# A gated convolution on one core: rows of T nine partitions apart, z in two blocks, output columns 8 bytes apart, three gate buffers

## The chip, the cores and the metric

The kernel runs on one core of a Trainium2 chip. The metric is the device time of one execution in microseconds. Three runs of the kernel before took 737.18 to 741.06 us, the median is 739.61 us. The profile is of one execution that took 739.31 us.

## What is computed

A softmax over seven taps gives, for each batch, position and head, the weights of a short causal filter over x. The filtered x goes through a gated block: a five-tap filter per channel and a sigmoid make the gate, one matrix product makes the value, and a second matrix product follows their product. x is 8 x 4224 x 192, with 8 heads of 24 channels; everything is float32, the three weights of the block come as float64.

```python
w = np.exp(weight_gen - np.max(weight_gen, axis=-1, keepdims=True))   # [B, S, H, 7]
w = w / (np.sum(w, axis=-1, keepdims=True) + 1e-09)
x_unf = x_pad[:, np.arange(S)[:, None] + np.arange(7)[None, :], :].reshape(B, S, 7, H, 24)
a = np.einsum('bshk,bskhg->bshg', w, x_unf).reshape(B, S, D)
gate_pre = np.zeros((B, S, D))
for k in range(5):
    gate_pre += conv_w[k][None, None, :] * ap[:, k:k + S, :]           # ap: a, 4 zero rows ahead
gate = 1.0 / (1.0 + np.exp(-gate_pre))
return gate * (a @ w_val) @ w_out
```

## The kernel before

The first filter is done on TensorE. For a group of 120 positions and one head and batch, the output is x (126 rows by 24 channels, held in 32 columns) times a band matrix T (126 rows by 120 positions) whose diagonals are the softmax weights. The sequence of 4224 positions is cut into 36 groups (88, 34 times 120, 56); pair 0 is the first group, pairs 1 to 17 are two groups each, pair 18 is the last group.

T is built by DMA. A `Softmax` part handles some 500 positions of all batches: weights are loaded into `wt` (`load`, L200), then max (L209), sub (L213) on VectorE (DVE), exp (L217) on ScalarE (ACT), sum, reciprocal and norm (L221 to L244) on DVE. `halo` (L236) copies the next rows' weights beside each partition's own, `spread` (L255) writes the taps on ACT into `zt`, and `store` (L261) writes rows with zeros behind them into a DRAM block `z`, cleared earlier by `clear` (L180). `load_t` (L299) reads from z with a row step that is a little shorter than the row, so that the band comes out slanted, one window of 16 rows at a time, into `tb`. x goes into `xt` by `load_x` (L278).

Per pair q, TensorE does: `bank` (L324), 8 banks of products for the two groups, into PSUM buffers `ps0` and `ps1`; then, for the pair before, the value product with the gate's half in four lines (`wvm_` L393, `wva_` L398, `wvd_` L401, `wvb_` L406); and for the pair before that the output product (`omA` L423, `omB` L432) into `ps3`, `ps1` and `ps2`. ACT evicts the banks to `ringA`, `ringB` and `S` (`evac`, L339), makes the gate's first tap (`tap0`, L365), the sigmoid (`sigm`, L374) and the output copies (`oev`, L441). DVE does the other taps (L369) and the product of gate and value (`gv`, L413 and L416). GpSimd (POOL) issues the small copies from S into holes of the rings (`move`, L347 and L349) and, from the third pair on, the x loads. SyncE (SP) issues the T loads, weights, halo, z and output stores.

Each engine works in order. The order is a table: `at(t, fn, ...)` gives a call a nominal time, and the calls are emitted in the order of these times. `when(q)` is the nominal start of pair q. Two `tb` buffers (one for each group of a pair), three `xt` buffers, and two gate buffers `aA`, `aB` set how far ahead work may run.

Of the kernel before, what the change touches and what calls it, by code (L numbers as in the profile page):

```python
# [16 lines left out]
def tile_dynconv_gated_moe(  # L17
# [245 lines left out]
    class Group:  # L263
# [16 lines left out]
        def segments(self):  # L280
            f = self.s - PAD
            for j in range(-(-self.k // G)):
                for i, p in enumerate(parts):
                    lo = max(G * j, p.use - f)
                    hi = min(G * j + G, self.k, ([q.use for q in parts] + [S])[i + 1] - f)
# [412 lines left out]
```

## Time and profile before

| | us |
|---|---|
| median of three runs | 739.61 |
| profiled execution | 739.31 |
| its span, first to last instruction | 737.5 |
| TensorE (PE) busy with matmuls | 556.2 (75%) |
| VectorE (DVE) busy | 417.4 (57%) |
| ScalarE (ACT) busy | 355.3 (48%) |
| GpSimd (POOL) busy | 186.4 (25%) |
| mean busy share of the 16 DMA engines, pairs 4 to 17 | 0.73 |

PE's share is an average over a start with long idle stretches and a steady part. In the rows below a line `L324 PE` is a group of matmuls, `PEld` the loads of their weights. A bracket behind a row of the timeline is the idle time of that engine just before it and what ended it. [...]

### The profile page before, as it was taken

The numbers are of one execution on the slowest core, as the hardware profiler recorded it, in microseconds if no ns is written. First come the engines' busy times: TensorE is split into PE (matmuls) and PEld (weight loads), VectorE is DVE, ScalarE is ACT, GpSimd is POOL, SyncE is SP. The second block draws the span as 40 slices with busy tenths as digits, with TensorE's granted clock in tenths as the row PEclk, the third lists the DMA queues.
The fourth block names the chain that finished last, engine by engine and source line by source line (L and its number), as shares of the span: only waits on it lengthen the run. The fifth ranks groups of instructions, "written<-read, shape, count | busy, mean of one in ns | idle before, by whom it ended". The sixth has DMA issues, their size and how long they took to land.

```text
span 737.5 us, 15169 instructions
## 1 busy us (share of the span) xinstructions
PE 556.2 (75%) x6444; PEld 443.5 (60%) x6444; DVE 417.4 (57%) x309; ACT 355.3 (48%) x433; POOL 186.4 (25%) x297
## 2 busy tenths in 40 slices
PE   4023503659689968996899995998699779999986
PEld 2022403447569666875587784767587658687675
DVE  3341351767367837692777455874587457836650
ACT  2321613625474556546564726374645474582432
POOL 9335210224040404040404312230314030403300
PEclk8556656779989988998999997999799979999989
DMA  8699696996856876787779692969388948873223
GB/s 260 123 217 200 162 209 170 209 219 104 231 107 173 186 205 121 195 163 191 138 198 178 187 226 53 206 133 258 97 182 158 253 88 182 191 201 82 61 81 99
DMA packets 67021, 123.47 MB, mean 167 GB/s; under 512 B 15625, under 2 KB 41684, under 8 KB 66954
## 3 DMA queue, kind: packets, MB, share of 16 engines
q1 hardware_dynamic: 52282, 90.29, 50.6%
q0 software_dynamic: 13936, 31.91, 21.0%
q8 instruction: 51, 0.84, 0.5%
q10 hardware_dynamic: 736, 0.32, 0.2%
q14 instruction: 16, 0.13, 0.1%
HBM read 60.83 MB, written 48.29 MB: 148 GB/s over the span
## 4 chain that ended last, share of the span: by engine, by line
PE 38%; DMA 28%; ACT 10%; issue 9%; SPq 6%; DVE 6%; POOL 2%; ACTq 0%; DVEq 0%; POOLq 0%
PE ps L423 11%; DMA wt<-in_weight_gen_dram 11%; PE ps L324 10%; DMA tb<-z 9%; PE ps L432 6%; SPq L299 5%; PE ps L398 4%; DMA xt<-in_x_dram 3%; ACT ot L441 3%; ACT aA L365 3%; ACT S L339 2%; PE ps L393 2%; DVE mx L209 2%; PE ps L401 2%; PE ps L406 2%
## 5 line engine op out<-in xcount | busy, mean ns | idle before, releaser
L324 PE MATMUL ps<-tb,xt 126*32 126x120 f32 (+2 forms) x4608 | 201.0, 340 | 170.0 <-DMA tb<-z 76.3
L324 PEld LDWEIGHTS ps<-tb,xt 126*32 126x32 f32 (+2 forms) x4608 | 180.3, 131 | 188.8 <-issue 80.5
L369 DVE SCALAR_TENSOR_TENSOR aA<-ringA,wf,aA 128x1920 f32<-128x1920 f32 (+2 forms) x76 | 158.0, 2079 | 137.1 <-ACT aA L365 135.2
L349 POOL DMA_DIRECT2D ringB<-S x76 | 42.3, 561 | 442.9 <-ACT ringB L339 424.5
L441 ACT COPY ot<-ps 120x768 f32<-120x768 f32 (+2 forms) x72 | 83.2, 1164 | 145.1 <-PE ps L432 73.7
L423 PEld LDWEIGHTS ps<-wf,aA 128*120 128x120 f32 (+2 forms) x576 | 130.3, 309 | 10.3 <-issue 7.3
L423 PE MATMUL ps<-wf,aA 128*120 128x192 f32 (+2 forms) x576 | 135.2, 388 | 0.7 <-DVE aA L413 0.7
L347 POOL DMA_DIRECT2D ringA<-S x152 | 82.1, 546 | 24.7 <-DMA ringB<-S 21.3
L369 DVE SCALAR_TENSOR_TENSOR aB<-ringB,wf,aB 128x960 f32<-128x960 f32 (+2 forms) x76 | 86.9, 1144 | 2.0
L432 PE MATMUL ps<-wf,aB 64*120 64x192 f32 (+2 forms) x576 | 76.6, 394 | 3.1 <-ACT ot L441 3.1
L209 DVE TENSOR_REDUCE mx<-wt 128x256 f32<-128x1792 f32 (+3 forms) x11 | 20.1, 1828 | 101.1 <-DMA wt<-in_weight_gen_dram 101.1
L432 PEld LDWEIGHTS ps<-wf,aB 64*120 64x120 f32 (+2 forms) x576 | 67.6, 302 | 15.9 <-ACT ot L441 7.9
L398 PE MATMUL ps<-ringA,wva 128*128 128x480 f32 (+2 forms) x144 | 61.8, 571 | 0.0
L255 ACT COPY zt<-wt 128x384 f32<-128x384 f32 (+6 forms) x44 | 39.1, 968 | 41.2 <-DMA wt<-wt 41.2
L413 DVE TENSOR_TENSOR aA<-ps,aA 128x960 f32<-128x960 f32 (+2 forms) x36 | 39.3, 1130 | 30.7 <-ACT ot L441 30.7
L365 ACT ACTIVATE aA<-ringA,wf 128x960 f32<-128x960 f32 (+2 forms) x38 | 50.3, 1326 | 9.8 <-DMA ringA<-S 9.7
L339 ACT COPY ringA<-ps 128x480 f32<-128x480 f32 (+2 forms) x72 | 37.8, 576 | 33.9 <-PE ps L324 33.9
L374 ACT ACTIVATE aA<-aA 128x1920 f32<-128x1920 f32 (+2 forms) x19 | 32.0, 1686 | 37.3 <-DVE aA L369 37.2
L398 PEld LDWEIGHTS ps<-ringA,wva 128*128 128x128 f32 x144 | 25.8, 189 | 36.2 <-issue 22.5
L217 ACT ACTIVATE wt<-wt 128x1792 f32<-128x1792 f32 (+3 forms) x11 | 16.4, 1493 | 41.0 <-DVE wt L213 40.9
L393 PE MATMUL ps<-ringA,wvm 128*32 128x480 f32 (+2 forms) x288 | 32.5, 560 | 0.9 <-ACT ot L441 0.9
L406 PE MATMUL ps<-ringB,wvb 64*128 64x480 f32 (+2 forms) x144 | 31.6, 555 | 0.0
(60 smaller groups left out, 387.7 us busy)
## 6 DMA issues: line engine op xcount, KB each, us to landing
out_dram<-ot SPq DMA_DIRECT2D x68, 360.0 KB
xt<-in_x_dram POOLq DMA_DIRECT2D x30, 768.0 KB, 10.4
tb<-z SPq DMA_DIRECT2D x208, 88.0 KB
z<-zt SPq DMA_DIRECT2D x8, 1152.0 KB
wt<-in_weight_gen_dram SPq DMA_DIRECT2D x16, 448.0 KB
z<-tb SPq DMA_DIRECT2D x2, 2944.0 KB
wt<-wt SPq DMA_DIRECT2D x9, 588.0 KB
ringA<-S POOLq DMA_DIRECT2D x136, 30.0 KB, 5.2
```

The costliest lines, as they stand in the source:

```text
L324: nc.tensor.matmul(out=pa[Q * c:Q * c + Q, n * l:n * l + n], lhsT=g.xb[0:k, LH * u + l, C * h:C * h + Q], rhs=g.t[0:k, u, PAD // 2:(PAD + ...
L339: nc.scalar.copy(out=dst, in_=pa)
L347: nc.gpsimd.dma_start(out=ringA[q:q + h, LH * u:LH * u + LH, p0:p0 + n], in_=St[p:p + h, :, 0:n])
L349: nc.gpsimd.dma_start(out=ringB[HD * u + q:HD * u + q + h, :, p0:p0 + n], in_=St[p:p + h, :, 0:n])
L365: nc.scalar.activation(out=self.acc(g)[:, ls], in_=self.src(g, 0)[:, ls], func=AF.Copy, scale=cw[:, g, 0:1])
L369: nc.vector.scalar_tensor_tensor(out=a, in0=self.src(g, j), scalar=cw[:, g, j:j + 1], in1=a, op0=ALU.mult, op1=ALU.add)
L393: nc.tensor.matmul(out=self.v2(e)[c:c + Q], lhsT=wvm[:, Q * i:Q * i + Q], rhs=self.A(e, u), start=True, stop=False, tile_position=(0, c))
L398: nc.tensor.matmul(out=self.v01(e)[:, u], lhsT=wva, rhs=self.A(e, u), start=True, stop=False)
L406: nc.tensor.matmul(out=self.v01(e)[:, u], lhsT=wvb[hs], rhs=self.Bt(e)[hs], start=False, stop=True, tile_position=(HD * u, 0))
L423: nc.tensor.matmul(out=ps[b][0:n, u, D * t:D * t + D], lhsT=g[:, u, 2 * k + t], rhs=woa, start=first and t == 0, stop=not first, skip_grou ...
L432: nc.tensor.matmul(out=ps[b][0:n, u, D * t:D * t + D], lhsT=g[hs, 2 * k + t], rhs=wob[hs], start=first and t == 0, stop=not first, skip_gr ...
L441: nc.scalar.copy(out=self.ot(e)[0:n, :, 2 * D * k:2 * D * k + 2 * D], in_=ps[b][0:n, :, 0:2 * D])
```

## The change

T's window becomes 14 rows, nine windows a group, and row i of window w goes to partition 9 i + w; x goes to the same partitions, by one DMA for each of the 8 batches. A cell of T (the weights of two positions for 4 batches and 8 heads) has 272 bytes for 256. The blocks in DRAM are two, each for one part at a time, of 64 x 8 rows for each half of the batches, and are cleared from a tile of zeros. The two halves of the batches lie on odd and even partitions in the softmax. There are three gate buffers, and `tap0` and the ring's halo stand in the pair's own stage. The banks run group by group. The two positions of an output product are neighbours, so that its weights' columns are 8 bytes apart for 16; an output store moves 1536 bytes a row for 3072. The table of times is new.

```diff
-    CELL = 2 * W
+    CELL = 2 * W + 4
+    HC2 = CELL // 2
-    G = 16
+    G, NW = 14, 9
...
-    tb = [const.tile([P, 2, CELLS, LH, H, 2], FP32, name=f"tb{i}") for i in range(2)]
+    tb = [const.tile([P, 2, CELLS, CELL], FP32, name=f"tb{i}") for i in range(2)]
...
-    aAs = [const.tile([P, L * 2 * NB], FP32, name=f"aA{i}") for i in range(2)]
-    aBs = [const.tile([P, LH * 2 * NB], FP32, name=f"aB{i}") for i in range(2)]
-    ots = const.tile([P, 2, 2, 4 * D], FP32, name="ot")
+    aAs = [const.tile([P, L * 2 * NB], FP32, name=f"aA{i}") for i in range(3)]
+    aBs = [const.tile([P, LH * 2 * NB], FP32, name=f"aB{i}") for i in range(3)]
+    ots = const.tile([P, 4, 2, 2 * D], FP32, name="ot")
...
+    ROWS = HD * RM
+    zb = [dpool.tile([(1 + 2 * ROWS) * PITCH], FP32, name=f"z{i}") for i in range(2)]
+    def clear_z(i, lo, hi, eng):
+        t, n = zb[i], (hi - lo) // P
+        for u in range(2):
+            dst = bass.AP(tensor=t.tensor, offset=t.offset + (1 + ROWS * u + lo) * PITCH,
+                          ap=[[n * PITCH, P], [PITCH, n], [1, PITCH]])
+            src = bass.AP(tensor=zero.tensor, offset=zero.offset, ap=[[zero.ap[0][0], P], [0, n], [1, PITCH]])
             eng.dma_start(out=dst, in_=src)
...
             src = bass.AP(tensor=wg.tensor, offset=wg.offset + (LH * u * S + self.r0) * ROW,
                           ap=[[R * ROW, HD], [S * ROW, LH], [1, R * ROW]])
-            eng.dma_start(out=self.wt[HD * u:HD * u + HD, :, 0:R].rearrange("p l r c -> p l (r c)"), in_=src)
+            w = self.wt[u:u + 1]
+            dst = bass.AP(tensor=w.tensor, offset=w.offset,
+                          ap=[[2 * w.ap[0][0], HD], [self.n * ROW, LH], [1, R * ROW]])
+            eng.dma_start(out=dst, in_=src)
...
+            if self.n == NB:
+                for j in range(L) if l is None else (l,):
+                    src = bass.AP(tensor=x.tensor, offset=x.offset + (f + j * S) * D, ap=[[D, G], [G * D, NW], [1, D]])
+                    eng.dma_start(out=self.xb[0:G * NW, j, 0:D], in_=src)
+                return
...
             src = bass.AP(tensor=b.t.tensor, offset=b.t.offset + off,
-                          ap=[[PITCH - W, hi - lo], [b.rows // 2 * PITCH, 2], [1, cells * CELL]])
+                          ap=[[PITCH - HC2, hi - lo], [ROWS * PITCH, 2], [1, cells * CELL]])
             c = (c0 + skip) * CELL
-            eng.dma_start(out=t[lo:hi, :, c:c + cells * CELL], in_=src)
+            d = t[NW * i0 + w:NW * i0 + w + 1, 0, c:c + 1]
+            dst = bass.AP(tensor=d.tensor, offset=d.offset,
+                          ap=[[NW * d.ap[0][0], hi - lo], [CELLS * CELL, 2], [1, cells * CELL]])
+            eng.dma_start(out=dst, in_=src)
...
-            g = self.aB[:, w * e:w * e + w].rearrange("p (c t) -> p t c", t=4)
+            g = self.aB[:, w * e + 2 * n * k:w * e + 2 * n * k + 2 * n].rearrange("p (c t) -> p t c", t=2)
...
-                    nc.tensor.matmul(out=ps[b][0:n, u, D * t:D * t + D], lhsT=g[hs, 2 * k + t], rhs=wob[hs],
+                    nc.tensor.matmul(out=ps[b][0:n, u, D * t:D * t + D], lhsT=g[hs, t], rhs=wob[hs],
...
-            order = [(gi, kind) for kind in (3, 2, 0, 1) for gi in range(ng)]
-            if q == 1:
-                order = [(gi, kind) for gi in range(ng) for kind in (3, 2, 0, 1)]
+            order = [(gi, kind) for gi in range(ng) for kind in (3, 2, 0, 1)]
...
+            for g in range(2):
+                st(14.8 if q else 8.0, pr.halo, g)
+            st(15.9 if q else 8.1, pr.tap0, 0, 0)
+            st(17.0 if q else 8.2, pr.tap0, 0, 1)
+            st(19.6 if q else 8.3, pr.tap0, 1)
...
-                    st(7.0 + 0.1 * gi, g.load_x, nc.sync if q < 2 else nc.gpsimd)
+                    if g.n == NB:
+                        st((0.0, 7.2)[gi], g.load_x, nc.gpsimd)
...
-                    tt = max(t + 7.2 + 0.1 * gi, p.ready + 0.001 * (1 + gi))
+                    tt = max(t + (3.5, 7.0)[gi], p.ready + 0.001 * (1 + gi))
...
-            st(0.0, p1.halo, 0)
-            st(0.01, p1.halo, 1)
-            st(0.02, p1.tap0, 0, 0)
-            st(1.0, p1.tap0, 0, 1)
-            st(2.6, p1.tap0, 1)
             for j in range(1, KC):
-                st(2.0 + 2.2 * (j - 1), p1.tap, 0, j)
-                st(10.8 + 1.2 * (j - 1), p1.tap, 1, j)
+                st((-2.5 if q > 1 else 0.0) + 2.1 * (j - 1), p1.tap, 0, j)
+                st(6.0 + 1.2 * (j - 1), p1.tap, 1, j)
```

On ACT, from the last output copy of one pair through the banks of the next, before; `aA0_76` and `aB0_78` are gate buffers, `ps0` to `ps3` PSUM buffers:

```order
L441 COPY ot_80<-ps2_91 120x2x384
L354 COPY ringA_73<-ringA_73 128x8x4
L354 COPY ringB_74<-ringB_74 128x4x4
L365 ACTIVATE aA0_76<-ringA_73,wf_86 128x960
L339 COPY S_75<-ps0_89 128x4x120
L365 ACTIVATE aA0_76<-ringA_73,wf_86 128x960
L339 COPY S_75<-ps0_89 128x4x120
L339 COPY ringB_74<-ps1_90 128x4x120
L365 ACTIVATE aB0_78<-ringB_74,wf_86 128x960
L339 COPY ringB_74<-ps1_90 128x4x120
L339 COPY ringA_73<-ps0_89 128x4x120 x2
L339 COPY ringA_73<-ps1_90 128x4x120 x2
```

The scaled copies L365 stand between the evictions L339. The same engine in the change, from the first output copy of a pair (L448 there) into the next pair's banks (L348); L374 is `tap0`, L216 exp:

```order
L448 COPY ot_82<-ps3_94 120x768
L374 ACTIVATE aA2_78<-ringA_73,wf_88 128x960 x2
L448 COPY ot_82<-ps3_94 120x768
L374 ACTIVATE aB2_81<-ringB_74,wf_88 128x960
L216 ACT_TABLE_LOAD
L216 ACTIVATE wt1_66<-wt1_66 128x4x448
L448 COPY ot_82<-ps1_92 120x768
L448 COPY ot_82<-ps2_93 120x768
L348 COPY S_75<-ps0_91 128x4x120
L348 COPY ringB_74<-ps0_91 128x4x120
L348 COPY ringA_73<-ps1_92 128x4x120 x2
```

The scaled copies have moved among the output copies of the stage before, and nothing but evictions is left in the banks.

On POOL before, the x loads of the two groups and the first moves of the next pair; the brackets hold the counts that each waits for, `DMASW0` to `DMASW7` being those of POOL's own DMAs:

```order
L278 DMA xt_72<-in_x_dram 128x8x192 [waits DMAHW6_49,DMASW0_49]
L278 DMA xt_70<-in_x_dram 128x8x192 [waits DMAHW2_49,DMAHW6_49,DMASW1_49,PE_49]
L349 DMA ringB<-S 8x4x240 [waits DVE_49,DMASW2_49,PE_49,Activation_49]
L349 DMA ringB<-S 8x4x240 [waits DMASW3_49,PE_49]
L349 DMA ringB<-S 8x4x240 [waits DMASW4_49]
```

In the change the same place on POOL, the eight x loads of a group and the first two moves behind them:

```order
L276 DMA xt_72<-in_x_dram 126x1x192 [waits DMASW3_49,PE_49]
L276 DMA xt_72<-in_x_dram 126x1x192 [waits DMASW4_49,PE_49]
L276 DMA xt_72<-in_x_dram 126x1x192 [waits DMASW5_49,PE_49]
L276 DMA xt_72<-in_x_dram 126x1x192 [waits DMASW6_49,PE_49]
L276 DMA xt_72<-in_x_dram 126x1x192 [waits DMASW7_49,PE_49]
L276 DMA xt_72<-in_x_dram 126x1x192 [waits DMASW0_49,PE_49]
L276 DMA xt_72<-in_x_dram 126x1x192 [waits DMASW1_49,PE_49]
L276 DMA xt_72<-in_x_dram 126x1x192 [waits DMASW2_49,PE_49]
L358 DMA ringB<-S 8x4x240 [waits DVE_49,DMASW3_49,PE_49,Activation_49]
L358 DMA ringB<-S 8x4x240 [waits DMASW4_49,PE_49]
```

A DMA takes the counter of the eighth one before it, and waits for that one's landing; 16 x loads a pair have come in where 2 were.

On SP before, the T loads for both groups of a pair, the weight load behind them, and a z store between output stores:

```order
L299 DMA tb_63<-z_95 16x2x512
L299 DMA tb_63<-z_95 16x2x704 x6
L299 DMA tb_63<-z_95 14x2x448
L299 DMA tb_64<-z_95 16x2x512
L299 DMA tb_64<-z_95 16x2x704 x6
L299 DMA tb_64<-z_95 14x2x448
L200 DMA wt_65<-in_weight_gen_dram 64x4x448 x2
L448 DMA out_dram<-ot 60x2x768 x2
```

In the change SP has, at the same place (L307 is `load_t`, L234 the halo, L199 the weight load, L262 the z store, L456 the output store):

```order
L307 DMA tb_63<-z_98 14x2x476
L307 DMA tb_63<-z_98 14x2x680 x7
L307 DMA tb_63<-z_98 14x2x476
L234 DMA wt_65<-wt_65 112x4x336
L234 DMA wt_65<-wt_65 14x4x336
L307 DMA tb_64<-z_98 14x2x476
L307 DMA tb_64<-z_98 14x2x680 x7
L307 DMA tb_64<-z_98 14x2x476
L199 DMA wt_66<-in_weight_gen_dram 64x4x448 x2
L262 DMA z_97<-zt 512x1x306 x2
L456 DMA out_dram<-ot 120x2x384 x4
```

The weight load still follows the T loads; these are 18 DMAs of 14 rows for 16 of 16, and the halo has moved between those of the two groups.

## Rows read from the trace of the kernel before

**Rows 1.** Windows: the four stages, then clean and slow pairs; columns as told above.
```profile
0.00:38.11 38.11, 7.63 (x37) 4.13 (x37) 12.80 (x26) 11.53 (x12) 22.67 (x29) 0.65 0.74 195
38.11:193.01 154.90, 77.56 (x1082) 61.69 (x1082) 72.73 (x57) 58.56 (x83) 40.86 (x60) 0.71 0.85 188
193.01:683.78 490.77, 427.43 (x4987) 343.02 (x4985) 309.55 (x204) 266.93 (x309) 116.38 (x196) 0.94 0.73 169
683.78:737.50 53.72, 43.57 (x344) 34.63 (x342) 22.29 (x22) 18.30 (x30) 6.48 (x12) 0.92 0.29 78
...
234.03:265.43 31.40, 29.77 (x359) 24.02 (x357) 20.08 (x13) 19.57 (x23) 8.37 (x14) 1.00 0.79 173
265.43:305.89 40.46, 31.66 (x358) 25.43 (x356) 26.64 (x18) 20.34 (x23) 8.34 (x14) 0.87 0.71 170
305.89:337.41 31.52, 29.85 (x359) 24.12 (x357) 19.56 (x13) 19.55 (x23) 8.36 (x14) 1.00 0.81 167
...
581.16:623.37 42.21, 32.32 (x359) 25.71 (x357) 26.60 (x18) 20.30 (x23) 8.35 (x14) 0.88 0.71 171
623.37:652.85 29.48, 29.14 (x359) 23.24 (x357) 18.59 (x13) 18.34 (x24) 8.35 (x14) 1.00 0.80 185
```
**Rows 2.** The chain that ended last, inside a slow pair: start, us, what.
```profile
255.90 11.97 DMA wt<-in_weight_gen_dram
```
**Rows 3.** Timeline of DVE in the same pair: start, us, engine, line, operation.
```profile
258.59 1.21 DVE L416 TENSOR_TENSOR aB<-ps,aB 128x480 f32<-128x480 f32 x2
267.96 2.07 DVE L209 TENSOR_REDUCE mx<-wt 128x256 f32<-128x1792 f32 x1 [8.16 <-DMA wt<-in_weight_gen_dram]
270.06 2.03 DVE L213 TENSOR_TENSOR wt<-wt,mx 128x1792 f32<-128x1792 f32 x1
```
**Rows 4.** Timeline of PE in the same pair, the waits within its banks.
```profile
274.56 3.67 PE L324 MATMUL ps<-tb,xt 126*32 126x120 f32 x64 [6.13 <-ACT ot L441]
280.91 5.62 PE L324 MATMUL ps<-tb,xt 126*32 126x120 f32 x128 [2.68 <-ACT S L339]
```
**Rows 5.** Timeline of PE, from a group's banks through a whole pair to the last banks.
```profile
659.87 4.54 PE L324 MATMUL ps<-tb,xt 126*32 126x120 f32 x128 [1.31 <-ACT S L339]
664.22 1.80 PE L393 MATMUL ps<-ringA,wvm 128*32 128x480 f32 x16
...
669.27 1.77 PE L401 MATMUL ps<-ringB,wvd 128*128 128x480 f32 x4
670.88 1.86 PE L423 MATMUL ps<-wf,aA 128*120 128x192 f32 x8
...
676.24 5.60 PE L423 MATMUL ps<-wf,aA 128*120 128x192 f32 x24
681.77 2.08 PE L432 MATMUL ps<-wf,aB 64*120 64x192 f32 x16
683.78 2.60 PE L324 MATMUL ps<-tb,xt 62*32 62x56 f32 x128
```
**Rows 6.** Lines by form, loads of weights: count | busy, mean ns | idle, releaser.
```profile
L423 PEld LDWEIGHTS ps<-wf,aA 128*120 128x120 f32 x544 | 125.0, 315 | 9.3 <-issue 6.4 <-DVE aA L413 1.2
L398 PEld LDWEIGHTS ps<-ringA,wva 128*128 128x128 f32 x144 | 25.8, 189 | 36.2 <-issue 22.5 <-ACT ringA L339 13.6
L393 PEld LDWEIGHTS ps<-ringA,wvm 128*32 128x32 f32 x288 | 10.0, 113 | 10.4 <-issue 9.0 <-ACT ot L441 1.1
L423 PEld LDWEIGHTS ps<-wf,aA 128*88 128x88 f32 x16 | 2.8, 238 | 0.6 <-issue 0.6
```
**Rows 7.** Windows in which T loads, z stores, and weight loads run.
```profile
390.00:396.00 6.00, 6.00 (x23) 3.04 (x16) 5.89 (x5) 1.88 (x2) 5.13 (x9) 1.00 1.05 152
409.00:412.00 3.00, 3.00 (x77) 2.94 (x72) 0.00 (x0) 3.00 (x4) 0.00 (x0) 1.00 1.08 379
436.00:440.00 4.00, 4.00 (x38) 3.57 (x40) 0.00 (x0) 0.00 (x0) 0.00 (x0) 1.00 1.07 215
```
**Rows 8.** DMA issues: names, queue, operation, count, KB each, median us to landing.
```profile
xt<-in_x_dram POOLq DMA_DIRECT2D x30, 768.0 KB, 10.4
```

More of the change, by code (lines that the diff above doesn't have):

```diff
@@ L280, in segments @@
         def segments(self):
             f = self.s - PAD
[L282 to L285, printed above, removed]
+            ends = [q.use for q in parts[1:]] + [S]
+            for w in range(-(-self.k // G)):
+                for p, e in zip(parts, ends):
+                    lo, hi = max(G * w, p.use - f), min(G * w + G, self.k, e - f)
@@ new lines, in tile_dynconv_gated_moe @@
+    at(4.9, s0.sub)
+    at(5.6, s0.exp)
+    at(6.2, s0.sum)
+    at(6.9, s0.recip)
+    at(7.0, s0.norm)
+    at(7.05, lambda: clear(tb[1], 1, 0, cs, nc.scalar))
+    at(7.1, s0.halo, (nc.sync, nc.scalar, nc.sync))
+    at(8.3, s1.max)
+    at(8.4, s1.sub)
+    at(8.5, s1.exp)
+    for i in range(4):
+        at(10.9 + 0.1 * i, s0.spread, i // 2, i % 2)
+    at(11.4, s0.store, (nc.sync, nc.scalar))
+    at(11.5, s1.sum)
+    at(11.6, s1.recip)
+    at(11.7, s1.norm)
+    at(11.8, s1.halo, (nc.sync,))
@@ L555, in tile_dynconv_gated_moe @@
     for i, f in enumerate(place_weights()):
[L556 removed]
+        at(25.0 + 0.35 * i, f)
     at(17.5, s2.max)
[L559 to L583 removed]
@@ L585, in tile_dynconv_gated_moe @@
-    at(26.0, b8[1].clear, nc.sync)
-    at(40.0, b8[0].clear, nc.sync)
-    J = 20.0
-    for i, p in enumerate(parts[3:]):
-        q = next(q.q for q in pairs if p.use < q.s + q.n)
-        if i == 0:
-            part_jobs(p, when(1) + 8.0, when(1) + 10.0, when(1) + 10.1, when(1) + 16.0, when(1) - 3.0)
-        else:
-            a = max(q - 4, 1)
-            part_jobs(p, when(a) + J, when(a + 1) + J, when(a + 1) + J + 0.1, when(a + 2) + J, when(a) + 14.0)
+    at(17.6, s2.sub)
+    at(17.7, s2.exp)
@@ new lines, in tile_dynconv_gated_moe, with jobs @@
+    at(24.0, s2.sum)
+    at(24.1, s2.recip)
+    at(24.2, s2.norm)
+    at(24.3, s2.halo, (nc.sync,))
+    for i in range(4):
+        at(31.0 + 0.1 * i, s2.spread, i // 2, i % 2)
+    at(32.0, s2.store, (nc.sync,))
+    at(33.0, clear_z, 1, 3 * P, 4 * P, nc.sync)
+    s0.ready, s1.ready, s2.ready = 11.4, 20.0, 32.0
+    def jobs(p, q):
+        a = max(q - 4, 1)
+        for u in range(2):
+            at(when(a) + (8.0 if q > 4 else 2.0), p.load, u, nc.sync)
+        for i, f in enumerate((p.max, p.sub, p.exp)):
+            at(when(a) + 20.6 + 0.1 * i, f)
+        for i, f in enumerate((p.sum, p.recip, p.norm)):
+            at(when(a + 1) + 20.6 + 0.1 * i, f)
+        at(when(a + 2) + 4.0, p.halo, (nc.sync,))
+        for i in range(4):
+            at(when(a + 2) + 8.0 + 0.9 * i, p.spread, i // 2, i % 2)
+        p.ready = when(a + 2) + 12.0
+        at(p.ready, p.store, (nc.sync,))
@@ L597, in tile_dynconv_gated_moe @@
+    for p in parts[3:]:
+        jobs(p, next(q.q for q in pairs if p.use < q.s - PAD + q.n))
     for q, pr in enumerate(pairs + [None, None]):
```

269 lines of the change are left out of this document (104 added, 165 removed).

## The prediction

> **What bounds the kernel now.** I read the stages first, then one slow and one clean pair, then what ends the waits in the slow one, and last the rates of TensorE's groups. The stages [rows 1] are: 38 us before the first bank, 155 us for pairs 0 to 3, 491 us for the fourteen pairs 4 to 17, 54 us of tail; they add to the span of 737.5 us, and the profiled execution took 739.3 us, 1.8 more, against a median of 739.6. In the steady stage TensorE is busy 427 of 491 us, DVE 310 and ACT 267, so TensorE is the engine to follow.
>
> The fourteen pairs are of two kinds. Eight clean ones take 29.5 to 31.5 us, six slow ones some 40 to 42 [rows 1]; three and two of them are shown. A slow one lies in [rows 2 to 4]. TensorE starts its banks at 265.43 and after two of them waits 6.13 us for ACT's copy L441, later another 2.68. ACT stands in its exp, which waits for DVE, and DVE idles 8.16 us before max (L209) for the weight load. The chain shows that load taking 11.97 us behind the T loads. Without this wait max would follow gv (L416) at once: the slow pair is a DMA stall passed on by two in-order queues. In the windows of [rows 7] all DMA engines are busy (share 1.0) yet the rate depends on what moves: T loads with ring moves 152 GB/s, weight loads 215, z stores 379.
>
> A clean pair without waits is the sum of [rows 5]: two groups of banks at 664.22 - 659.87 = 4.35 us each, 8.7; from L393 at 664.22 to the next bank at 683.78, 19.56. Together **28.3 us**; the clean pairs take 1 to 3 us more, the waits inside their banks for ACT, which runs the scaled copies (tap0, L365) between the evictions.
>
> **The change, part by part.**
>
> *T rows nine partitions apart, cells of 272 bytes.* A window's rows (16 before, 14 now) sat in adjacent partitions; now nine apart. The bytes barely change: 2 x 126 rows x 2 x 2816 B = 1.42 MB a pair, now 2 x 126 x 2 x 2720 = 1.37. At 152 GB/s that is 9.3 us of full DMA; the best rate in the rows, 379, would make it 3.6. I take 300, between them and nearer the stores, whose rows also lie over all partitions: 4.6 us. The window of 152 holds ring moves too, so part of its slowness isn't T's. [...]
>
> *Bank order by group.* Before, the two groups of a pair alternate, so both T buffers come free at the end of the banks. Now the first group ends after four banks, and its next T loads start 4.4 us earlier; the weight load follows the T loads on SP in both kernels. Then T, weights (0.9 MB at 215 to 379 GB/s: 2.4 to 4.3 us, their rows now interleaved over all partitions) and half of x fit between bank end and max: 8.7 + 4.6 + 4.3 ends 18 us into the pair. Before, gv ended 258.59 + 1.21 - 234.03 = 25.8 us into it [rows 1, 3]; with the savings below it ends near 22. The 8.16 us of idle go to nought. What is late next: ACT. In a pair with exp, max and sub (2.07 + 2.03) [rows 3] still lie between gv and exp, and the four zt copies before the first output copy; I charge such a pair 3.5 us over a clean one, between 0 and the present 10.
>
> *x by batch.* Eight DMAs of 126 rows for one of 128 x 8, on POOL. POOL issues 28 DMAs a pair instead of 14. The order of the program shows that each waits on one of eight counters in turn, so a DMA can't be issued before the eighth one ahead has landed: a pair needs at least 28/8 x landing time. The 768 KB x loads landed in 10.4 us [rows 8]; pieces an eighth as large will land sooner, from 2 us to that 10.4, so 7 to 36 us a pair. I take 5, 17.5 us, covered by the pair; that cover is gone above 7.5 us.
>
> *Three gate buffers, tap0 a stage earlier.* tap0 leaves the banks' evictions; the 1 to 3 us of waits in the banks go. It now stands behind the first output copies, some 20 us into the pair (8.7 + 676.24 - 664.22 [rows 5]), and needs the ring moves there, which are issued after the evictions, from 9 us on. That cover of 10 us is what it costs nothing by; without it ACT waits ahead of the copies that free TensorE's buffers.
>
> *Output columns 8 bytes apart.* The weights of L423 and L432 are gate columns; they were 16 bytes apart. L423 takes 5.53 / 24 = 0.230 us an instruction, L432 2.01 / 8 = 0.251 a pair that runs side by side [rows 5]. Streaming alone would be 192 columns at L401's rate (1.61 / 4 / 480 = 0.84 ns a column): 0.161. So the weight load limits. The loads themselves [rows 6]: contiguous, 189 ns for 128 columns and 113 for 32, 0.8 ns a column; 16 bytes apart, 315 for 120 and 238 for 88, 2.4 a column. At 8 bytes no row shows one. The bounds are nothing and 32 x (0.230 - 0.161) + 16 x (0.251 - 0.161) = 2.2 + 1.4 = 3.6 us a pair. I take 3.0: halfway in spacing already leaves the load under 0.161, since half of 2.4 ns x 120 is 0.144. [...]
>
> *z in two blocks.* Clears fall from 1 + 128 x (2 + 4 + 6 + 8 + 8) rows of 2944 B, 10.6 MB, to two blocks of 1025 rows of 2856 B, 5.9. At the stage's 188 GB/s [rows 1] the 4.7 MB are 25 us of a stage whose DMA share is 0.85. The T loads of pairs 1 to 4 (5.6 MB) save 4 x 4.7 = 19 more. Softmax 0's sum also no longer stands behind softmax 1's max. All of it together is 44 us if DMA alone sets the start. Against it, exp of softmax 2 now stands ahead of pair 0's evictions on ACT, and DVE takes over the weight conversions from POOL. I take pair 4's start from 193 to 148, bounds 135 and 175.
>
> **The sum.** A clean pair 28.3 - 3.0 + 0.5 = 25.8 us, six with exp 29.3: 8 x 25.8 + 6 x 29.3 = 382, from 491 (the 0.5 is what is left of the waits in the banks, an estimate between 0 and the present 1). The tail: two and a half pairs' outputs, 7 us, and tap0 earlier, 2: 45. 148 + 382 + 45 + 1.8 = **577 us**, against the profiled 739.3 and so against the median. DVE (310 / 14 = 22.1 a pair) and ACT (19.1) stay under 25.8, DVE closely. DMA has T 1.4, x 1.5, output 1.5 and the softmax parts' 1.5 MB a pair: 20 us at 300 GB/s.
>
> **The rivals.**
> (1) The spacing gives nothing, if a load's time depends on its columns alone. Then each pair is 3.0 us longer and the tail 6: 577 + 42 + 6 = 625. For it: no row has 8 bytes. Against: the two slopes of [rows 6]. [...]
> (2) Supply still ends the waits: the weight load is late as now, because T, x and stores now fill the DMA engines earlier too. Six pairs at 37 instead of 29.3: 577 + 46 = 623. For it: the share of 1.0 in all of [rows 7]. Against: the earlier start and the rates above.
> (3) The start isn't shortened, since there the chain through halo, zt and z decides: 577 + 45 = 622. For it: the share of 0.85 leaves room for such a chain. Against: the fewer bytes shorten the chain's own transfers too.
> (4) Slower than before: POOL's counters decide. Every pair then lasts 3.5 times the landing time of a POOL DMA. To reach 739 the pairs must take (739 - 148 - 45 - 2) / 14 = 38.9 us, a landing of 11.1 us for all 28; at 13 us it would be 14 x 45.5 + 195 = 832. For it: x took 10.4 us in large pieces. Against: the ring moves in the same queue are small, and two large loads in flight carried as many bytes as sixteen small ones.
> (5) The T loads aren't faster (152 GB/s stays): they end 4.7 us later, still before gv; the start loses 19: 596.
>
> **How the numbers follow.** Forecast with (5) 0.63, (1) 0.12, (2) 0.09, (3) 0.08, (4) 0.04, and 0.04 for several gains missing at once, 660 to 737. Range: the low end takes the bounds 135 for the start, 3.6 us for the spacing and 1 us for exp: 577 - 13 - 8 - 15 = 541 for all three at once, so 545; the high end takes in (1), (2) and (3), each with 20 us to spare: 645. A measurement can tell about 0.5% of this kernel's time from no change: faster 0.94, same 0.02, slower 0.04.
>
> **What would show it.** Pair starts 25 to 30 us apart from pair 4 on, with no wait of TensorE on L441's successor above 3 us; L423's successor at 0.165 us and its loads near 190 ns; T stretches above 250 GB/s; no DVE idle before max on the weight load; POOL's x loads landing under 7 us; pair 4 starting before 175. It is wrong if TensorE's waits are for x or for T in the steady stage, if the second-group weights still take 315 ns, or if pairs 0 to 3 still take 190 us.

## The result and the profile after

The changed kernel takes 612.38 us (median of four runs, 611.49 to 613.28), the kernel before 740.34 beside it: a ratio of 0.828, 95% interval 0.825 to 0.831. The forecast was 577 with a range of 545 to 645. The time lies in the range, 35 us above the forecast, and those 35 us are what the experiments below had to find.

The profiled execution has a span of 611.5 us. Its windows, in the columns of [rows 1], which hold start and end, their distance in us, the busy time and the number of instructions of PE, PEld, DVE, ACT and POOL, the granted clock as a share of full speed, the busy share of the DMA engines, and GB/s: the four stages, then a pair with a softmax halo and exp in it and the pair behind it without.

```profile
0.00:40.42 40.42, 8.35 (x43) 4.63 (x43) 20.57 (x23) 12.01 (x11) 26.79 (x41) 0.69 0.75 215
40.42:165.38 124.96, 69.70 (x1082) 53.30 (x1083) 78.32 (x69) 58.95 (x88) 62.04 (x105) 0.75 0.64 182
165.38:570.52 405.14, 353.12 (x4988) 269.10 (x4992) 291.22 (x200) 224.50 (x304) 214.59 (x374) 0.94 0.71 200
570.52:611.50 40.98, 34.42 (x342) 24.97 (x342) 18.65 (x21) 14.68 (x25) 6.49 (x12) 1.00 0.37 102
287.06:320.19 33.13, 25.87 (x358) 19.43 (x356) 22.46 (x16) 17.45 (x24) 17.83 (x31) 0.90 0.87 240
320.19:345.81 25.62, 23.93 (x358) 18.09 (x357) 21.52 (x16) 16.49 (x22) 16.04 (x28) 1.00 0.62 172
```

Against [rows 1] the start up to pair 4 went from 193.0 to 165.4 us, the fourteen pairs from 490.8 to 405.1, the tail from 53.7 to 41.0. There are still two kinds of pairs: eight clean ones of 23.8 to 26.7 us (mean 25.3, before 29.5 to 31.5) and six slow pairs of 31.7 to 37.9 (mean 33.8, before 40.4 to 42.2). Before, a slow pair was 10 us above a clean one; now it is 8.6.

What a slow pair waits for is another thing than before. Timeline of PE in pair 6, which starts at 228.34, and two rows of the clean pair behind it:

```profile
253.66 1.64 PE L442 MATMUL ps<-wf,aB 64*120 64x192 f32 x8 [5.78 <-ACT ot L448]
255.23 5.32 PE L433 MATMUL ps<-wf,aA 128*120 128x192 f32 x24
265.06 5.42 PE L333 MATMUL ps<-tb,xt 126*32 126x120 f32 x192 [1.16 <-ACT ot L448]
...
281.46 4.17 PE L433 MATMUL ps<-wf,aA 128*120 128x192 f32 x24
285.56 1.57 PE L442 MATMUL ps<-wf,aB 64*120 64x192 f32 x16
```

TensorE waits 5.78 us for an output copy, and the products right behind the wait run slower (5.32 us for 4.17; the granted clock is 0.50 from 255.23 to 257.00 and 0.85 to 0.90 over each of the six slow pairs). Such a wait, of 5.0 to 6.6 us, stands in all six slow pairs. The copy's story is in the timelines of ACT, DVE and SP of the same pair. In SP's, the second number is the time from the first to the last issue of a row's DMAs:

```profile
239.90 1.80 ACT L383 ACTIVATE aA<-aA 128x1920 f32<-128x1920 f32 x1 [1.36 <-DVE aA L378]
248.07 3.73 ACT L253 COPY zt<-wt 128x512 f32<-128x512 f32 x4 [6.37 <-DMA wt<-wt]
251.71 1.00 ACT L383 ACTIVATE aB<-aB 128x960 f32<-128x960 f32 x1
252.83 0.78 ACT L448 COPY ot<-ps 120x768 f32<-120x768 f32 x1
```
```profile
228.89 2.03 DVE L242 TENSOR_TENSOR wt<-wt,mx 128x1792 f32<-128x1792 f32 x1
258.51 2.02 DVE L208 TENSOR_REDUCE mx<-wt 128x256 f32<-128x1792 f32 x1 [4.55 <-DMA wt<-in_weight_gen_dram]
```
```profile
232.07 8.19 SPq L307 DMA_DIRECT2D tb<-z  x9
240.36 1.54 SPq L234 DMA_DIRECT2D wt<-wt  x2
242.01 8.32 SPq L307 DMA_DIRECT2D tb<-z  x9
250.37 1.40 SPq L199 DMA_DIRECT2D wt<-in_weight_gen_dram  x2
251.87 1.72 SPq L262 DMA_DIRECT2D z<-zt  x2
```

Read from the bottom: DVE's norm (L242) ends at 230.9, and the softmax halo (L234) could go. It stands on SP behind nine T loads, goes at 240.4 and lands at 248.1; ACT waits 6.37 us for it, copies zt for 3.7 us and comes to the output copy at 252.8. Nine more issues later the weight load goes, lands at 258.5, and DVE's max waits 4.55 us for it. An issue of a T load keeps SP for about 0.8 us, 18 of them for 16.5 us of a pair. Durations of single issues, in ns, least, median, most; the first row is of the kernel after, the second of the kernel before, the third of the run e4 below:

```profile
L307 SPq DMA_DIRECT2D tb<-z x320: 676/789/1938, 33.3 to 554.6; - x160
```
```profile
L299 SPq DMA_DIRECT2D tb<-z x288: 263/414/6523, 32.8 to 665.1; - x144
```
```profile
L307 SPq DMA_DIRECT2D tb<-z x320: 258/385/2007, 34.0 to 531.8; - x160
```

The change has nearly doubled what an issue costs. The transfers themselves did get faster: a full T packet took 240 ns in the median before (2816 bytes; mean 242) and takes 114 after (2720 bytes; mean 154). But the loads of a pair now go out over 18 us (232.07 to 250.33), where before sixteen went out in 9.48. The issues aren't all of it: the DMA engines are busy 0.46 of the time while the first nine go out, 0.91 while the halo is under way (240.36 to 248.07) and 0.95 while the weights are (250.37 to 258.51), so both are late to go and slow to land.

### The profile page after: what moved, and what is told of

Its sections match the earlier page's. It is cut to its first block, busy times and chain, and to the rows that moved or that the text cites. A ratio compares the mean times of both kernels' runs of the same rounds, so it can differ in the third digit from the quotient of the medians.

```text
span 611.5 us, 15672 instructions
## 1 busy us (share of the span) xinstructions
PE 465.6 (76%) x6450; PEld 352.0 (58%) x6450; DVE 408.8 (67%) x311; ACT 310.1 (51%) x427; POOL 309.9 (51%) x532
## 4 chain that ended last, share of the span: by engine, by line
PE 34%; DMA 19%; SPq 15%; issue 13%; POOL 8%; DVE 6%; ACT 4%; POOLq 0%; ACTq 0%; DVEq 0%
SPq L307 12%; PE ps L333 11%; PE ps L433 8%; DMA wt<-in_weight_gen_dram 5%; PE ps L442 5%; PE ps L407 4%; DMA z<-zt 4%; POOL xt L276 3%; POOL ringA L356 3%; DVE aA L378 3%; DMA xt<-in_x_dram 3%; DMA wt<-wt 2%; PE ps L402 2%; PE ps L410 2%; PE ps L415 2%
## 5 line engine op out<-in xcount | busy, mean ns | idle before, releaser
L333 PE MATMUL ps<-tb,xt 126*32 126x120 f32 (+2 forms) x4608 | 142.2, 282 | 98.0 <-DMA tb<-z 40.1
L333 PEld LDWEIGHTS ps<-tb,xt 126*32 126x32 f32 x4608 | 132.6, 115 | 108.1 <-issue 78.9
L276 POOL DMA_DIRECT2D xt<-in_x_dram x264 | 157.2, 623 | 25.8 <-DMA ringA<-S 7.0
L358 POOL DMA_DIRECT2D ringB<-S x76 | 42.2, 560 | 223.4 <-ACT ringB L348 184.4
L433 PE MATMUL ps<-wf,aA 128*120 128x192 f32 (+2 forms) x576 | 110.5, 348 | 0.0
L433 PEld LDWEIGHTS ps<-wf,aA 128*120 128x120 f32 (+2 forms) x576 | 102.0, 200 | 13.6 <-issue 13.2
L448 ACT COPY ot<-ps 120x768 f32<-120x768 f32 (+2 forms) x72 | 55.7, 798 | 85.0 <-PE ps L442 53.1
L442 PE MATMUL ps<-wf,aB 64*120 64x192 f32 (+2 forms) x576 | 65.0, 356 | 37.6 <-ACT ot L448 37.6
L442 PEld LDWEIGHTS ps<-wf,aB 64*120 64x120 f32 (+2 forms) x576 | 48.7, 193 | 56.7 <-ACT ot L448 46.4
L253 ACT COPY zt<-wt 128x512 f32<-128x512 f32 (+5 forms) x40 | 34.2, 924 | 54.1 <-DMA wt<-wt 33.0
L348 ACT COPY ringA<-ps 128x480 f32<-128x480 f32 (+2 forms) x72 | 36.2, 556 | 27.3 <-PE ps L333 27.3
L407 PEld LDWEIGHTS ps<-ringA,wva 128*128 128x128 f32 x144 | 26.3, 193 | 40.0 <-issue 22.5
L374 ACT ACTIVATE aA<-ringA,wf 128x960 f32<-128x960 f32 (+2 forms) x38 | 37.5, 1031 | 14.5 <-DMA ringA<-S 14.5
L348 ACT COPY S<-ps 128x480 f32<-128x480 f32 (+2 forms) x36 | 19.9, 552 | 46.2 <-PE ps L333 46.1
L425 DVE TENSOR_TENSOR aB<-ps,aB 128x480 f32<-128x480 f32 (+2 forms) x36 | 21.5, 637 | 20.8 <-ACT aB L383 20.8
```

The costliest lines, as they stand in the source:

```text
L276: eng.dma_start(out=self.xb[0:G * NW, j, 0:D], in_=src)
L333: nc.tensor.matmul(out=pa[Q * c:Q * c + Q, n * l:n * l + n], lhsT=g.xb[0:k, LH * u + l, C * h:C * h + Q], rhs=t[:, u, PAD // 2:(PAD + n) / ...
L348: nc.scalar.copy(out=dst, in_=pa)
L358: nc.gpsimd.dma_start(out=ringB[HD * u + q:HD * u + q + h, :, p0:p0 + n], in_=St[p:p + h, :, 0:n])
L407: nc.tensor.matmul(out=self.v01(e)[:, u], lhsT=wva, rhs=self.A(e, u), start=True, stop=False)
L433: nc.tensor.matmul(out=ps[b][0:n, u, D * t:D * t + D], lhsT=g[:, u, t], rhs=woa, start=first and t == 0, stop=not first, skip_group_check= ...
```

## The experiments

All runs but e5 start from the changed kernel, each with the edit that its diff or its heading tells, and each was timed beside the kernel before.

**e1: the halo ahead of the T loads on SP.**

```diff
-        at(when(a + 2) + 4.0, p.halo, (nc.sync,))
+        at(when(a + 2) + 3.4, p.halo, (nc.sync,))
```

> The softmax halo is issued on SP ahead of the nine T loads of the next pair's first group, not behind them. Theory A (SP's issue queue): the halo was ready to go at 230.9 us in pair 6 but stood behind nine issues of 0.8 us each until 240.4, and landed at 248.1, so ACT's zt copies and behind them the output copy came late. Now it goes at about 231, the waits of PE on the output copy (5.0 to 6.3 us in five pairs) and the half clock after them (about 1.1 us) vanish, the T loads start 1.6 us later: slow pairs of about 28 us for 33, the time 612 - 25 = 587 us. Rival B (the DMA engines are full and the halo lands near 247 wherever it is issued): slow pairs of 32 to 33 us, 605 to 612.

Measured: 617.19 us (609.9 to 619.5), ratio 0.834 (0.826 to 0.841), no gain. Yet the wait was taken away where theory A said: in the pair from 232.8 to 258.2 the wait at that output copy is 0.64 us, and that pair takes 25.4. The pair behind it, from 258.2, now waits in its banks instead. PE, DVE and SP there:

```profile
258.19 1.95 PE L333 MATMUL ps<-tb,xt 126*32 126x120 f32 x64
268.93 7.65 PE L333 MATMUL ps<-tb,xt 126*32 126x120 f32 x192 [8.79 <-ACT ot L448]
```
```profile
262.38 2.02 DVE L208 TENSOR_REDUCE mx<-wt 128x256 f32<-128x1792 f32 x1 [8.61 <-DMA wt<-in_weight_gen_dram]
```
```profile
235.43 2.12 SPq L234 DMA_DIRECT2D wt<-wt  x2
237.65 16.23 SPq L307 DMA_DIRECT2D tb<-z  x18
253.92 1.41 SPq L199 DMA_DIRECT2D wt<-in_weight_gen_dram  x2
```

The weight load behind the 18 issues is late next: it goes at 253.9 and lands at 262.4, exp waits for max and sub, and the last two output copies wait behind exp. Both theories missed the time; the wait went as A said, and its price isn't to be had alone.

**e2: the weight load a pair earlier.** In some parts the load overwrites weights of the part before last that aren't spread yet, so those rows of z hold other numbers.

```diff
-            at(when(a) + (8.0 if q > 4 else 2.0), p.load, u, nc.sync)
+            at(when(a) + (8.0 - TP if q > 6 else 8.0 if q > 4 else 2.0), p.load, u, nc.sync)
```

> The weight load of a softmax part stands a whole pair earlier on SP (behind the T loads of the clean pair before), all else as in the changed kernel. Theory A: DVE's wait for this load (about 4.5 us in a slow pair) delays exp and the last two output copies, which costs PE 1.1 to 2.5 us at the next banks; that goes: 612 - 6 = 606, the halo's wait stays. Rival (the late weight load is what makes the pairs slow, as in the kernel before): the slow pairs fall to 27, 612 - 30 = 582.

Measured: 607.21 us, ratio 0.824 (0.818 to 0.830). That is theory A's 606, though by time alone it can't be told from the changed kernel's 0.828 (0.825 to 0.831); the trace bears it out. Max no longer waits; the output copy is still waited for in every slow pair (2.8 to 6.3 us), here in pair 6:

```profile
257.24 1.64 PE L442 MATMUL ps<-wf,aB 64*120 64x192 f32 x8 [5.87 <-ACT ot L448]
```

The slow pairs stay at 33.9 us in the mean, and the six clean pairs right behind them get shorter by 0 to 2.9 us, 1.2 in the mean.

**e9: both at once, the load behind the copies that free its buffer.**

```diff
-        at(when(a + 2) + 4.0, p.halo, (nc.sync,))
+        at(when(a + 2) + 3.4, p.halo, (nc.sync,))
...
+        tl = max(when(a) + 8.0 - TP, when(first[i - 2] + 2) + 11.2)
         for u in range(2):
-            at(when(a) + (8.0 if q > 4 else 2.0), p.load, u, nc.sync)
+            at(tl if q > 6 else when(a) + (8.0 if q > 4 else 2.0), p.load, u, nc.sync)
```

> Rows still nine apart; the halo ahead of the T loads as in the run of it alone, and the weight load a pair earlier or right behind the copies that free its buffer. The halo alone took the wait at the output copy away (0.6 us was left of 5.8) and gave 8.8 us of wait for the weight load, which then stood behind 18 T issues. Theory (both stand behind SP's issues, and each alone hides the other): the slow pairs fall to 26 to 28 us: 612 - 5 x 6 = 582, to 575. Rival (SP's issuing of 23 us in a pair is too much wherever a step stands, T loads or output stores come late next): 600 or more.

Measured: 584.37 us, ratio 0.791 (0.787 to 0.796). From pair 5 on no pair is above 29.5 us, most are at 25 to 27. The window of pairs 5 to 17, 26.3 us each:

```profile
201.10:542.50 341.40, 318.05 (x4630) 241.53 (x4628) 265.74 (x185) 206.74 (x282) 198.56 (x346) 0.99 0.74 215
```

Where e1 gave nothing and e2 5 us, together they give 28, with the same transfers and the same issues: two steps behind one queue hid each other.

**e4: T's rows in adjacent partitions, and x's with them.** This undoes the first words of the title.

```diff
-                    src = bass.AP(..., ap=[[D, G], [G * D, NW], [1, D]])
+                    src = bass.AP(..., ap=[[D, G * NW], [1, D]])
...
-            d = t[NW * i0 + w:NW * i0 + w + 1, 0, c:c + 1]
+            d = t[lo:lo + 1, 0, c:c + 1]
-                          ap=[[NW * d.ap[0][0], hi - lo], [CELLS * CELL, 2], [1, cells * CELL]])
+                          ap=[[d.ap[0][0], hi - lo], [CELLS * CELL, 2], [1, cells * CELL]])
```

> A window's fourteen rows of T go to adjacent partitions again (and x in the same order), with all else as changed. Two effects are to be told apart. Theory A (rate of the transfer): a T packet takes about 246 ns for 114, T's 1.37 MB a pair need some 9 us more of full DMA in 25 and the banks wait for T: 630 to 650. Theory B (issue): an issue of a T load on SP takes about 0.41 us for 0.79, SP has 7 us a pair less to do, the halo and the weight load go out earlier: 590 to 605. The issue's median in the trace tells whether the strided target is what makes it longer.

Measured: 596.07 us, ratio 0.808 (0.803 to 0.813): without the nine-apart rows the kernel is 16 us faster. Theory B. An issue takes 385 ns (third row of issues above), a T packet about 220 ns, near the 240 of before; the wait at the output copy in pair 6 falls from 5.78 to 4.11 us, and DVE's for the weight load from 4.55 to 3.51. SP and PE in that pair:

```profile
226.90 5.06 SPq L307 DMA_DIRECT2D tb<-z  x9
232.06 1.65 SPq L234 DMA_DIRECT2D wt<-wt  x2
233.81 8.81 SPq L307 DMA_DIRECT2D tb<-z  x9
```
```profile
246.60 1.64 PE L442 MATMUL ps<-wf,aB 64*120 64x192 f32 x8 [4.11 <-ACT ot L448]
```

The halo stands behind 5.06 us of issues for 8.19. The second nine still take 8.81 us, where nine times 385 ns would be 3.5; what the rest is spent on isn't in these rows. So shorter issues are a part of the cure; the slow pairs fall to 31.7 us in the mean, 2.1 less. While the T loads go out (226.9 to 241.8) the DMA engines are busy 0.74 of the time, in the changed kernel (232.07 to 250.3) 0.71, before (387.96 to 397.5) 0.93: on this mean the slower packets find room. An x load's issue on POOL also got shorter (536 ns for 623 in the mean); what of the 16 us is x's was not run apart.

**e10: e9's two moves with adjacent rows.**

> The same two moves with T's rows in adjacent partitions, where an issue takes 0.39 us for 0.79 and a packet 224 ns for 114. Theory (SP's queue decides, and DMA still has room in a pair): no wait above 2 us in the steady pairs, 14 x 25.3 + 163 + 42 + 2 = 561. Rival (the slower packets now set the supply, and T or x comes late): 580 to 596.

Measured: 571.75 us (567.9 to 578.6), ratio 0.773 (0.767 to 0.779), 13 us under e9. The mean of pairs 4 to 17 is 26.2 us, with no wait of TensorE on an output copy above 2.2. It misses the 561 in two places, read from a profiled execution that took 7 us over the median: the fourteen pairs are 13 us over 14 x 25.3, and pair 4 starts at 169.1 for 163, behind a wait for T:

```profile
169.13 9.81 PE L333 MATMUL ps<-tb,xt 126*32 126x120 f32 x256 [7.47 <-DMA tb<-z]
```

**e6: the start.** Every other T load of pair 1 goes on ACT's queue.

```diff
-                    at(tt, g.load_t, p, w, lo, hi, nc.sync)
+                    at(tt, g.load_t, p, w, lo, hi, (nc.sync, nc.scalar)[w % 2] if q < 1 else nc.sync)
```

> The changed kernel with every other T load of pair 1 issued on ACT's queue instead of SP's; nothing else. Theory A (SP's issuing ends the waits of the start: 19 us of issues between 59 and 78 us stand ahead of pair 1's banks and of the next halo and weight load): pair 1 starts some 8 us earlier, at 66 for 73.7, and everything after it: 612 - 8 = 604. Rival (the halo, zt and z chain of the parts decides): pair 1 starts earlier, and pair 4 where it did: 610 to 613.

SP's issues for pair 1 in the changed kernel, then in this one:

```profile
59.12 19.43 SPq L307 DMA_DIRECT2D tb<-z  x18
```
```profile
58.22 12.34 SPq L307 DMA_DIRECT2D tb<-z  x10
```

Measured: 607.09 us, ratio 0.823 (0.816 to 0.830). Pair 1 starts at 68.9 for 73.7 and pair 4 at 160.6 for 165.4: what is won stays won. It is 5 us, 0.6 of theory A's. The intervals of the two ratios overlap, so the timing alone can't tell it; the traces agree with it.

**e11: e10 with three more moves in the start:** e6's, the weight load behind the z store, and max, sub and exp of a part ahead of the sum and norm of the one before (20.3 for 20.6).

> The run with adjacent rows, halo and weight load moved (572), with three more moves in the start: every other T load of pair 1 on ACT's queue, the weight load behind the z store instead of ahead of it, and max, sub and exp of a part ahead of the sum and norm of the one before. Theory (the start's waits add up along one chain): pair 1 some 3 us earlier, pair 3's wait for exp 4 us shorter and pair 4's for T 3 us: 572 - 10 = 562. Rival (each is hidden by another wait of the start): 568 to 574.

Measured: 570.21 us (563.0 to 572.3, six runs), ratio 0.771 (0.767 to 0.775); beside e10's 0.773 no difference can be told. Pair 4 starts 7.5 us earlier (161.6) but takes 30.2 us for 26.4. Its steady stage, one clean pair, and the longest pair in it:

```profile
161.59:526.90 365.31, 343.93 (x4987) 259.54 (x4987) 288.44 (x199) 226.82 (x307) 202.41 (x374) 0.99 0.86 220
217.10:242.47 25.37, 24.29 (x358) 18.07 (x356) 23.71 (x17) 17.66 (x25) 15.72 (x30) 1.00 0.95 236
318.70:349.80 31.10, 26.88 (x359) 19.37 (x357) 22.97 (x16) 17.39 (x24) 17.24 (x33) 0.89 0.96 257
```

TensorE is busy 344 of 365 us there, and the DMA engines' share has gone from 0.71 to 0.86: this is now near both. It is the fastest of the versions by median, 42 us under the changed kernel.

**e3: columns 16 bytes apart again** (the old `omA`, `omB`, `oev` and `store`, with `ots` in two halves):

```diff
-            g = g.rearrange("p u (c t) -> p u t c", t=2)
+            g = ....rearrange("p u (c t) -> p u t c", t=4)
...
-                    nc.tensor.matmul(..., lhsT=g[:, u, t], rhs=woa,
+                    nc.tensor.matmul(..., lhsT=g[:, u, 2 * k + t], rhs=woa,
```

> The output columns go back to 16 bytes apart, with the old output tile and rows of 3072 bytes. Theory A: the loads of the weights of an output product take 0.31 us for 0.20 and the products 0.230 and 0.251 us for 0.174 and 0.196: 32 x 0.056 + 16 x 0.055 = 2.7 us a pair. All of it shows in the clean pairs and the tail, and in the part of the slow pairs that follows the wait: 12 x 2.7 + 7 = 39, or 651. Rival (SP and DMA set the pace in every pair): under 625.

Measured: 645.03 us, ratio 0.875 (0.869 to 0.882): the spacing, with the output stores that go with it, is worth 33 us in this kernel, by the traces 24 in the fourteen pairs and 7 in the tail. Loads of weights by form, of the changed kernel and of e3 (where L433 is L432):

```profile
L433 PEld LDWEIGHTS ps<-wf,aA 128*120 128x120 f32 x544 | 97.6, 203 | 12.0 <-issue 12.0
L442 PEld LDWEIGHTS ps<-wf,aB 64*120 64x120 f32 x544 | 46.5, 195 | 54.3 <-ACT ot L448 44.9 <-issue 9.4
```
```profile
L432 PEld LDWEIGHTS ps<-wf,aA 128*120 128x120 f32 x544 | 129.8, 315 | 9.8 <-issue 8.0
```

**e5: the kernel before with the 8-byte columns alone** (the same lines the other way round).

> The kernel before with one part of the change alone: output columns 8 bytes apart, with the new output tile and four stores a pair (they go from 60 rows of 3072 bytes to 120 rows of 1536). Theory (the spacing is worth the weight load's time wherever TensorE sets the pace): 2.7 us in each of the eight clean pairs and in what follows the stall of the six slow ones, some 14 x 2.5 = 35, and 5 in the tail: 739 - 40 = 699. Rival (in this kernel the weight load and DMA set the pace of the slow pairs, and the shorter output rows slow DMA): 715 to 739.

Measured: 721.30 us, ratio 0.977 (0.972 to 0.983): 17 us, at the rival's end. The products take what they take after the change (4.17 us for 24, 1.57 for 16), so TensorE has 2.7 us a pair less to do. But of this the fourteen pairs show 7 us in all, and the tail 7: the clean pairs fall only from a mean of 30.6 to 30.3. TensorE comes to its banks sooner and waits there for ACT, which runs tap0 among the evictions: the banks' idle time put down to output copies and evictions of S is 48.2 + 47.1 us in all, before 38.5 + 37.1. In the changed kernel, whose banks hold no tap0, the same edit is worth twice as much (e3); that tap0's place is the reason is argued and not run, and e7 shows a second one, that output copies are slowed in banks with cells of 256 bytes (2.38 us in the median inside the banks of the kernel before, 0.80 outside).

**e7: cells of 256 bytes.**

```diff
-    CELL = 2 * W + 4
+    CELL = 2 * W
```

> The changed kernel with cells of T of 256 bytes for 272, all else as changed. Theory A (SP's issuing and not the bytes sets the supply): T packets get 6% smaller, nothing waits less: 609 to 613. Rival B (the 16 bytes more keep TensorE's reads of T or the writes of the rows apart): the banks take longer than 3.4 to 3.7 us a group, by at least 5%: 612 + 19 x 0.4 = 620 or more. No trace so far has 272 and 256 beside each other with all else equal.

Measured: 656.67 us (651.8 to 664.2), ratio 0.888 (0.884 to 0.893): the 16 bytes of padding are worth 44 us, the largest price of the parts that were run apart. The profiled execution took 664.2 us, 8 over the median, so a per cent of what follows may be that execution's. Timelines of DVE, ACT and PE around the banks that start at 304.52:

```profile
305.11 3.75 DVE L242 TENSOR_TENSOR wt<-wt,mx 128x1792 f32<-128x1792 f32 x1
```
```profile
303.99 3.82 ACT L448 COPY ot<-ps 120x768 f32<-120x768 f32 x2 [1.67 <-PE ps L442]
```
```profile
304.52 9.81 PE L333 MATMUL ps<-tb,xt 126*32 126x120 f32 x254
```

The same work in the changed kernel, at a place with no wait in the banks:

```profile
227.80 1.50 ACT L448 COPY ot<-ps 120x768 f32<-120x768 f32 x2 [1.66 <-PE ps L442]
```
```profile
546.70 7.17 PE L333 MATMUL ps<-tb,xt 126*32 126x120 f32 x256
```

The norm takes 3.75 us beside the banks for 2.03 (above), two output copies 3.82 for 1.50, the banks 9.81 for 7.17. So it isn't only TensorE: what DVE and ACT run while TensorE reads T in 256-byte steps is slowed; the banks' idle time put down to output copies is 14.0 us in all for 7.8. Not all work suffers alike: over the whole trace an output copy takes 1.25 us in the mean for 0.80, the norm 3.21 for 2.02, an eviction of S 0.61 for 0.56. In the changed kernel the output copies take 0.81 inside and 0.80 outside. Outside the banks nothing changed (four taps of 960 elements 4.97 us in both).

The kernel before, whose cells have 256 bytes, shows it too: 2.38 us for an output copy inside the banks (median of 15), 0.80 outside. The first wait of [rows 4], 6.13 us, ended with two such copies, which take 1.50 us above:

```profile
273.73 3.57 ACT L441 COPY ot<-ps 120x768 f32<-120x768 f32 x2
```

**e8: the two groups' banks in turn, and e12: two gate buffers.** In e8 the next pair's T loads stand ahead of the first group's last bank in the program, and that bank is computed from the next pair's rows; in e12 tap0 overwrites gate values that output products of the same stage still are to read.

```diff
-            order = [(gi, kind) for gi in range(ng) for kind in (3, 2, 0, 1)]
+            order = [(gi, kind) for kind in (3, 2, 0, 1) for gi in range(ng)]
```

> The changed kernel with the two groups' banks alternating as before. Theory (the first group's buffer comes free some 2.5 us later, SP's 18 issues and all that stands behind them start later by that): the five slow pairs take 2 to 3 us more, and in the clean pairs, where SP ends about as late as TensorE, 0 to 1: 612 + 15 = 627, within 618 to 640. Rival (the order of the banks is worth nothing, the halo waits for DVE anyway): 610 to 614.

```diff
-    aAs = [const.tile([P, L * 2 * NB], FP32, name=f"aA{i}") for i in range(3)]
+    aAs = [const.tile([P, L * 2 * NB], FP32, name=f"aA{i}") for i in range(2)]
...
-            self.aA = aAs[q % 3][:, 0:L * self.n]
+            self.aA = aAs[q % 2][:, 0:L * self.n]
```

> The changed kernel with two gate buffers for three, the order of the work unchanged. Theory (tap0 in the pair's own stage writes the buffer that the output products of that stage still read): ACT's first scaled copy waits for the last of the products that read the half, and the output copies behind it wait with it; TensorE waits some 3 to 5 us more in every pair: 612 + 16 x 4 = 676. Rival (the third buffer isn't needed for this order): 612.

Measured: 745.47 us for e8, 614.46 for e12 (ratio 0.833, 0.829 to 0.838). Neither settles what it was meant to. e8's time is that of its own flaw: TensorE waits for a T load in the middle of every pair's banks (8.36 us in the one at 282). e12 shows that the third buffer saves no wait in this order; what it buys is that the order may be used at all. What the order of the banks is worth by itself stays open, and so does the z in two blocks, which was not run apart.

## Why the prediction came out 35 us low

**The clean pairs: right, 25.3 us for 25.8, in part by luck, since errors cancel.** From L402 to the next banks the pair at 320.19 takes 345.81 - 329.02 = 16.79 us; forecast 19.56 - 3.0 = 16.56. The banks had been left at their 8.7 us [rows 5] and take 7.1; the waits in them, forecast 0.5, are 1.7 in that pair.

**Output columns: right.** L433 takes 4.17 / 24 = 0.174 us, L442 1.57 / 8 = 0.196, from 0.230 and 0.251 [rows 5]: 32 x 0.056 + 16 x 0.055 = 2.7 us a pair for the 3.0 taken, and e3 shows them as 33 us of the kernel's time. The loads fell to 203 ns, not to the 144 that halfway would give. Rival (1) is out: the same 120 columns take 203 ns at 8 bytes and 315 at 16.

**The six exp pairs: wrong, 33.8 us for 29.3, which is 27 of the 35 us.** The step that failed is "The 8.16 us of idle go to nought", and with it the 3.5 us charged for a pair with exp, which came to 8.6. The idle before max fell only to 4.55 us in pair 6, and ahead of it ACT, named as late next for its zt copies, met a wait of 6.37 for the halo that those copies read. The halo had been noted as moved in between the T loads of the two groups on SP, and no price was put on that. What decides is a duration that the sum had no term for: SP's issue of a T load, 0.41 us in the trace of before and 0.79 now. Eighteen of them are 14 us; the five rows of SP above hold 21.2 us of a slow pair, and four output stores follow. That the place behind these issues is the cause is shown by e9, which moves two steps, leaves all transfers as they are and brings 28 us; e4 shows that the length of an issue is a part of it. In price this is rival (2), 623, and in part its mechanism: the engines are busy 0.71 of the time while T goes out, but 0.91 and 0.95 while the halo and the weights are under way. Yet e9 ends the waits with the same bytes, so it was the order that let them decide.

**T's faster rows: the sign was wrong.** The forecast had 4.6 us of transfer at 300 GB/s for 9.3. The packets did go from 240 to 114 ns, the pair's loads from 9.5 to 18 us. Rival (5) looked for a loss of rate; the loss is in the issue. As placed here, rows nine apart cost 16 us (e4), and with the two moves of e9 they still cost 13 (e10). The packets alone went the way that was forecast, 114 ns nine apart and about 220 adjacent (e4); no term of the sum priced the issue.

**The start: 165 us for 148, within its bounds of 135 and 175; 17 of the 35 us.** It gained 28 of the 45. The chain that ended last between 36 and 166 us runs through weight load, max, sub, exp, zt and z, then SP's T issues, then halo, zt and z again. The T issues, which the sum had no term for, are a quarter of it (24.9%), and e6 takes 5 us of that back with one line. So rival (3) is half of it: a chain decides, but one with SP's issues in it. Shorter issues alone don't do it: with an issue half as long pair 4 starts at 163.2 (e4), only 2 us earlier. Where the other 12 us of the 17 went stays open.

**Cells of 272 bytes: the largest miss, and it doesn't show in the total.** They were costed by their bytes, and the padding is worth 44 us (e7). The sum stood by luck: it took the banks' 8.7 us from the trace of before, where the cells of 256 bytes slow them (in e7 9.81 us for 7.17), and charged nothing for the work that the new order puts beside them. There the signs were to be seen and not read: banks of 4.35 us a group [rows 5], which now take 3.6, and output copies of 2.38 us inside the banks for 0.80 outside.

**x by batch and POOL's counters: right.** An x load lands in 4.0 us (5 taken), so rival (4), the slower one, was far from deciding:

```profile
xt<-in_x_dram POOLq DMA_DIRECT2D x264, 94.5 KB, 4.0
```

**The tail: right,** 41.0 us for 45.

The sum of the misses in the windows: start +17, exp pairs 6 x 4.5 = +27, clean pairs 8 x -0.5 = -4, tail -4, which makes 36 for the profiled execution; the median lies 1 us under it.

## What to carry to other kernels

Cost the issue of a DMA as work of the queue that issues it: count times the issue's own duration, and again after a change of its access pattern, since the same bytes took twice as long to issue here (789 ns for 385, e4). What somebody waits for goes ahead of bulk loads on such a queue, and where two awaited steps stand behind the same bulk, move both, or the second hides what the first gave (here nothing and 5 us singly, 28 together). A padding that looked like waste was worth 44 us here (e7): compare the durations of other engines' instructions while an operand is read with those of the same instructions elsewhere.
